# Part products of a pair interleaved with the v products of an older block

## The chip, the cores and the metric

The kernel runs on one core of a Trainium2 chip. The core has five engines, each with its own queue of instructions, which it runs in order: TensorE (PE, matrix products; PEld is its weight load), VectorE (DVE), ScalarE (ACT), GpSimd (POOL) and SyncE (SP), which issues most of the DMAs, in the order of its queue. Times are device microseconds; the metric is the median over several runs of the whole program.

## The reference

The input x has 2048 rows of 512. The result is x plus two branches on the normalized rows:

```python
xn = _layernorm(x, axis=-1)
return x + _A_ref(xn, dft matrices) + _B_ref(xn, w_q, k1, k2, u, v)
# A: y = Real(DFT_seq(DFT_hidden(xn))), by the matrices given as inputs
# B: 32 heads; each takes the best 2 of 64 x 64 = 4096 experts by product keys (k1, k2)
act = _gelu(jnp.einsum("nd,nhkd->nhk", xf, ue))      # ue = u[top_e]
out = jnp.einsum("nhk,nhk,nhkd->nd", g, act, ve)     # ve = v[top_e], g = softmax of the two scores
```

Branch B is computed densely: for every row the products with all 4096 experts, multiplied by a gate matrix that is zero except where an expert was taken.

## The kernel before, in words

The first 420 us hold branch A, the routing and the preparation of u and v (both split into two f16 parts, so that each product takes three matmuls). What the change touches begins there. It runs over 16 blocks b of 128 rows. For each block there are three kinds of work:

- **z**: the u products of the block with all 4096 experts, then gelu, into a tile of activations `act` (128 x 4096, 32 bit). Three such tiles exist, blocks take them in turn (b modulo 3).
- **G and W**: the gate. `g_prep` (lines 1283, 1288, 1291) makes one-hot factors L (1.2 us) and R (two rows of 0.4 us) on DVE for 16 of the 128 rows at a time, from a compacted table `cmp` that ACT makes from a transpose read from memory (line 948); three pairs of L and R rotate. `g_mm` (1299) multiplies them on PE, 32 matmuls for each half, two halves a G, four G a block. `w_part` (1307, 1312, 1313) multiplies activation and gate on DVE, has ACT (or, with `here=True`, DVE itself by the CAST in line 1310) round that to f16 and DVE subtract to get the second part; the result W lies in the place of the activations.
- **v**: 16 v tiles, each six matmuls of 128x512 (line 1357), all into one PSUM bank. Nine v tiles stay on the chip, seven stream through three places (`v_load`, 1333); `v_order` says in which order a block takes its 16, so that the last streamed ones serve the next block first.

Blocks 0 and 1 compute z plainly (`u_part`, 1108). From block 2 on, two blocks (a pair) share a scheme of seven products in place of eight, for each of four quads a to d of experts: 28 **slots** of 24 matmuls (1186), in the order `SEQ`. A slot "6b" is product 6 of quad b. Products 1, 6, 7 and 4 of a quad use one PSUM bank X one behind the other, 5 and 3 use Z, 2 uses Y. After each, an eviction moves or adds the bank into an activation tile: 1, 5 and 6 by ACT copies (1225, 1230, 1232), 2, 3 and 7 by DVE adds (1227, 1235, 1238), 4 by gelu on ACT (1215), with further gelus a few slots later. A slot that adds to a bank must wait for the eviction before it. Four PSUM banks are shared by all of these and by the v sums. Products 6, 3 and 7 need sums of u parts, 512 KB each, that come from memory through a **ring** of three tiles (`ring_load`, 1169). `ring_plan` decides with a model clock (1344 ns a slot) which load goes behind which slot.

The order of work is written out: `phases` is z0, z1, v0, then for each pair z(b, b+1), v(b-1), v(b), and last v15. `put(phase, place, ...)` hangs G, W, factor preparation and the rest onto places of these phases. Of the 28 slots of a pair three go into the end of v(b-2), 24 stand in a phase of their own, one goes into the start of v(b-1). Through all of this run jobs that check the input matrices: 68 **comparisons**, each two loads on SP (1395 and 1396, together 512 KB into a tile `cx`), some DVE rows from line 1411 to 1449 and sums on ACT (1382, 1385), and 35 smaller ones; they are spread over the places from place 3 (`first`) on. A scheduler then places each instruction in its engine's queue by this order and its own estimate of when inputs are there, so that an instruction of a later phase can stand ahead of one of an earlier phase. At the end of each block `finish` adds the v sum to y; `store`, `load_y` and `add_x` are its transfers. A variant called `safe` for other inputs exists and doesn't run here.

Of the kernel before, what the change touches and what calls it, by code (L numbers as in the profile page):

```python
# [18 lines left out]
P = 128  # L19
# [17 lines left out]
def tile_fnet_peer(ctx, tc, x, ca, cb, c5, wt, wf, wr, wq, kt, ut, vn, out):  # L37
# [683 lines left out]
    def part_b(safe, stS, stP, stQ, stE, xt, u_sb, cmp_p, w4):  # L721
# [471 lines left out]
        def z_pair(b, n):  # L1193
# [3 lines left out]
            total = len(SEQ) - BEFORE - BEHIND  # L1197

            def work(at):

                if at < len(SEQ):
# [3 lines left out]
                    op, qd = o[0], turn_q(o[1], n)  # L1205
# [39 lines left out]
            def middle(after):  # L1245
                cg = 0
                for k in range(total):
                    work(BEFORE + k)
                    while cg < 16 and (k + 1) * 16 >= (cg + 1) * total:
                        after(cg)  # L1250
                        cg += 1

            def behind(k):
                work(BEFORE + total + k)
                while k + 1 == BEHIND and late:
                    late.pop(0)[1]()

            return work, middle, behind
# [76 lines left out]
        def v_part(b, pv, cg):  # L1335
            w16 = parts(b)
            if b + 1 == NT and cg == 7 and not safe:
# [559 lines left out]
```

## Time and profile before

| | |
|---|---|
| median of 3 runs | 1145.69 us (1144.38 to 1147.01) |
| profiled execution | 1152.65 us, its span 1150.9 us |
| mean granted TensorE clock | 0.987 |
| z of block 0 and 1 | 418.5 to 483.5 us |
| from the first to the last v product | 483.5 to 1144.5 us |
| DMA traffic of the whole span | 220.5 MB, mean 192 GB/s |

PE is busy for 96% of the span and DVE for 83%. Busy time is a share over stages with different limits; where PE idles, the list of waits names what came last. The granted clock is 1 nearly everywhere; it is lower behind long idle times of PE. "issue" as a releaser means that the profile shows nothing that the engine waited for.

### The profile page before, as it was taken

How to read it: one execution, taken by the hardware profiler on the slowest of the kernel's cores; microseconds unless marked ns; L12 is line 12 of the kernel's file. 1: busy time of each engine (PE TensorE's matmuls, PEld its weight loads, DVE VectorE, ACT ScalarE, POOL GpSimd, SP SyncE). 2: the span in 40 equal slices, each digit the busy share in tenths (PEclk: the TensorE clock that was granted, in tenths of full speed). 3: DMA queues.
4: the chain of work that ended last, by engine and by line, in shares of the span. 5: the costliest groups of instructions: out<-in, count | busy, mean ns of one | idle time of the engine just before them, and what ended most of it. 6: DMA issues, size and time to landing. Idle time of an engine off the chain costs nothing. (4 is left out here: it accounts for less than half of the span.)

```text
span 1150.9 us, 29229 instructions
## 1 busy us (share of the span) xinstructions
PE 1109.5 (96%) x11528; PEld 724.9 (63%) x11528; DVE 959.2 (83%) x2840; ACT 682.2 (59%) x1226; POOL 333.2 (29%) x385
## 2 busy tenths in 40 slices
PE   9999999999999998599999998999998999999997
PEld 6455554544544468469569568669568659659643
DVE  7899789999989895767978877879988879879892
ACT  6558598889787582246547535546636546636530
POOL 1429999889887840000000000000000000000000
PEclk8999999999999999799999999999999999999999
DMA  9883546456344328438658656757756857747743
GB/s 299 258 222 145 191 140 218 123 196 183 112 127 129 98 82 206 122 124 285 206 187 276 198 192 232 259 176 264 230 174 231 279 177 235 256 146 235 207 129 114
DMA packets 132274, 220.52 MB, mean 192 GB/s; under 512 B 35092, under 2 KB 71067, under 8 KB 132126
## 3 DMA queue, kind: packets, MB, share of 16 engines
q1 hardware_dynamic: 129520, 214.28, 57.7%
q0 software_dynamic: 2304, 4.20, 2.3%
q8 instruction: 92, 1.51, 0.5%
q14 instruction: 56, 0.46, 0.1%
q10 hardware_dynamic: 302, 0.08, 0.0%
HBM read 183.06 MB, written 29.69 MB: 185 GB/s over the span
## 5 line engine op out<-in xcount | busy, mean ns | idle before, releaser
L252 PE MATMUL s<-m,xq 128*128 128x512 f16 x1344 | 297.4, 379 | 1.4 <-ACT ss L962 1.4
L1357 PE MATMUL v<-v,act 128*128 128x512 f16 x1044 | 233.1, 379 | 0.7 <-DVE act L1313 0.7
L252 PEld LDWEIGHTS <-xq 128*128 128x128 f16 x1344 | 129.7, 98 | 152.5 <-issue 2.7
L1370 POOL DMA_DIRECT2D y<-in_x_dram x16 | 14.4, 898 | 687.2 <-DVE L L1283 253.9
L1357 PEld LDWEIGHTS <-act 128*128 128x128 f16 x1044 | 99.3, 98 | 113.9 <-DVE act L1313 1.2
L1186 PEld LDWEIGHTS <-u 128*128 128x128 f16 x2688 | 156.5, 98 | 15.7 <-issue 9.3
L1283 DVE TENSOR_TENSOR L<-io_lam,cmp 128x2048 f16<-128x2048 f16 x128 | 154.8, 1214 | 12.1 <-PE g L1299 11.9
L966 DVE MAX8 vals<-ss 128x8 f32<-128x64 f32 x896 | 133.3, 216 | 5.5 <-ACT ss L962 5.2
L1186 PEld LDWEIGHTS <-s 128*128 128x128 f16 x1944 | 110.8, 98 | 2.2 <-DMA s<-s_d 2.1
L1357 PE MATMUL v<-v,w 128*128 128x512 f16 x480 | 107.6, 379 | 0.0
L1382 ACT ACTIVATE cx<-cx 128x896 f32<-128x896 f32 x68 | 64.3, 945 | 64.0 <-DVE cx L1430 43.9
L1312 ACT ACTIVATE act<-g 128x1024 f16<-128x1024 f32 x36 | 46.9, 1314 | 86.4 <-DVE g L1307 85.4
L970 DVE FIND_INDEX8 idx<-vals,ss 128x8 uint16<-128x256 f32 x224 | 93.8, 419 | 0.0
L962 ACT ACTIVATE ss<-s,wsc 128x512 f32<-128x512 f32 x120 | 80.2, 681 | 22.4 <-PE s L252 12.7
L1186 PE MATMUL z<-xb,u 128*128 128x128 f16 x1344 | 84.5, 219 | 5.5 <-ACT act L1215 4.5
L1186 PE MATMUL z<-x,u 128*128 128x128 f16 x1344 | 85.4, 221 | 2.2 <-DVE act L1235 1.1
L1186 PE MATMUL z<-x,s 128*128 128x128 f16 x1296 | 81.2, 219 | 1.8 <-DMA s<-s_d 1.8
L1299 PE MATMUL g<-R,L 128*128 128x32 f16 x2048 | 62.4, 176 | 20.2 <-DVE cx L1446 16.6
L1299 PEld LDWEIGHTS <-L 128*128 128x128 f16 x2048 | 60.0, 96 | 30.5 <-DVE cx L1446 16.8
L1357 PEld LDWEIGHTS <-w 128*128 128x128 f16 x480 | 45.6, 98 | 51.4
L1215 ACT ACTIVATE act<-act,scl 128x512 f32<-128x512 f32 x56 | 40.0, 719 | 54.5 <-DVE act L1235 23.6
L1307 DVE SCALAR_TENSOR_TENSOR g<-act,scl,g 128x1024 f32<-128x1024 f32 x44 | 55.8, 1281 | 11.8 <-ACT act L1215 11.8
(360 smaller groups left out, 1900.8 us busy)
## 6 DMA issues: line engine op xcount, KB each, us to landing
v<-v_d SPq DMA_DIRECT2D x67, 512.0 KB, 4.3
s<-s_d SPq DMA_DIRECT2D x63, 512.0 KB, 3.9
cx<-in_cb_dram SPq DMA_DIRECT2D x64, 448.0 KB, 6.0
w<-in_wq_dram SPq DMA_DIRECT2D x28, 512.0 KB, 5.9
fit<-in_wq_dram SPq DMA_DIRECT2D x28, 512.0 KB, 6.3
uv<-in_vn_dram SPq DMA_DIRECT2D x16, 512.0 KB
uv<-in_ut_dram SPq DMA_DIRECT2D x16, 512.0 KB, 3.6
s_d<-v SPq DMA_DIRECT2D x32, 256.0 KB, 2.5
```

Source lines behind the costliest of these rows:

```text
L252: nc.tensor.matmul(ps, xt[i][:, l, kd, :], m[:, r, kd, :], start=(n == 0), stop=(n == 3 * KD - 1))
L962: nc.scalar.activation(s, ps, AF.Copy, scale=inv)
L966: nc.vector.max(vals[:, i, w, :, h], s[:, g, :])
L970: nc.vector.max_index(idx[:, i, w].rearrange("p k h -> p (k h)"), vals[:, i, w, 0:2].rearrange("p k h -> p (k h)"), s[:, w * HC:g + 1, :]. ...
L1186: nc.tensor.matmul(bank[:, t * P:(t + 1) * P], lt, rt, start=(t == k == 0 and op in "125"), stop=(t == 3 and k == 5), skip_group_check=op ...
L1215: nc.scalar.activation(d, d if src is None else src, AF.Gelu_apprx_tanh, scale=zsc)
L1283: pin(nc.vector.tensor_tensor(L.rearrange("p t (l two) -> p t l two", two=2), io_lam.rearrange("p (l two) -> p l two", two=2).unsqueeze(1) ...
L1299: nc.tensor.matmul(p[:, hf, t * NC:(t + 1) * NC], L[:, t, :], R[:, t, :], start=True, stop=True)
L1307: nc.vector.scalar_tensor_tensor(w, act[:, :, ts], fw, w, op0=ALU.mult, op1=ALU.mult)
L1312: nc.scalar.activation(w16[..., 0], w, AF.Copy)
L1357: nc.tensor.matmul(pv, w16[:, c, :, l], v_sb[g][:, r, cc, :], start=(n + cc == 0 and k == 0), stop=(n == end and cc == 1 and k == 2))
L1382: pin(nc.scalar.activation(f, f, AF.Abs, accum_out=chk[:, n:n + 1]))
```

## The change

- `SEQ` has a new order, in which 6, 3 and 7 of a quad stand close together, and the quads are taken in one order for all pairs.
- The phases are z0, z1, then for each pair a combined phase ("a", b) with all 28 slots of the pair and, between them, the 16 v tiles of block b-2 (`TILES` says ahead of which slot each tile goes, `TILES0` for the first pair), then v(b-1); at the end v14 and v15. The first two tiles of v(b-1) go ahead of the last slot.
- The three activation tiles are allocated once. Block b+1 of a pair takes the tile of block b-2, whose v products run in the same phase; `v_order` is written so that a tile's part of `act` has been used when a slot writes there. The new order of v also changes when the streamed v tiles are loaded: v tile 9 is sixth in odd blocks.
- The model clock of the ring is 2000 ns a slot, which gives 84 loads in place of 66.
- G, W and the preparation have new places; no W uses the CAST on DVE any more. The jobs start at place 10 in place of 3, with 28 places in a combined phase and 2.2 and 2.8 us as lengths.
- `store`, `load_y`, `add_x` and the loads for the next pair (`fetch`) have new places.

The counts of PE's matmuls are the same. In the changed file most lines here are a few numbers lower (1283 is 1274, 1288 is 1279, 1291 is 1282, 1299 is 1290, 1307 is 1298, 1357 is 1352, 1333 is 1324, 1413 is 1407); 1169 is 1170.

```diff
+        AT = [a.tile([P, NC, P], F32, tag="act", name=f"act{n}") for n, a in enumerate(ap)]
+        AT.append(w4.rearrange("p (c n) -> p c n", n=P))
+
         def act_tile(b):
-            if b % 3 == 2:
-                return w4.rearrange("p (c n) -> p c n", n=P)
-            return ap[b % 3].tile([P, NC, P], F32, tag="act", name=f"act{b}")
-
-        BT = [act_tile(b) for b in range(2)]
+            return AT[b % 3]
+
...
-            SEQ = ("1a 5a 2a 6a 1b 3a 2b 7a 5b 6b 1c 4a 3b 7b 2c 5c 6c 1d 4b 3c 7c 5d 2d 6d 4c 3d 7d 4d").split()
-            BEFORE, BEHIND = 3, 1
-
-            def turn_q(k, n):
-                return ((0, 3, 2, 1), (1, 3, 2, 0))[n % 2]["abcd".index(k)]
+            SEQ = ("1a 5a 2a 6a 3a 7a 1b 4a 5b 2b 6b 3b 7b 1c 4b 5c 2c 6c 3c 7c 1d 4c 5d 2d 6d 3d 7d 4d").split()
+            TILES = [1, 2, 3, 3, 4, 6, 8, 10, 11, 13, 15, 17, 18, 20, 22, 24]
+            TILES0 = [0, 0, 0, 0, 0, 0, 0, 1, 3, 5, 8, 11, 14, 17, 20, 23]
+
+            def turn_q(k):
+                return (0, 3, 2, 1)["abcd".index(k)]
...
-                    ns = 1344
+                    ns = 2000
                     if OPS[o[0]][1] is not None:
-                        USES.append((clock, clock + ns, turn_q(o[1], n), OPS[o[0]][1]))
+                        USES.append((clock, clock + ns, turn_q(o[1]), OPS[o[0]][1]))
                     clock += ns
-                clock += 50000
+                clock += 22000
...
+                    if at + 1 == len(SEQ):
+                        while late:
+                            late.pop(0)[1]()
+
+            return work
...
-        VO = [None if n in (1, 3, 5, 7, 9, 12, 14) else 0 for n in range(16)]
-        res, ext = iter(range(V2)), iter(range(V2, 16))
-        VO = [next(ext if v is None else res) for v in VO]
-
         def v_order(b):
-            return VO if b % 2 else VO[::-1]
+            if b % 2:
+                return [15, 13, 11, 7, 6, 9, 5, 4, 3, 2, 1, 0, 8, 14, 12, 10]
+            if b < 14:
+                return [10, 12, 14, 8, 0, 1, 2, 3, 4, 5, 6, 7, 9, 11, 13, 15]
+            return [10, 12, 14, 8, 0, 1, 2, 9, 3, 4, 5, 6, 7, 11, 13, 15]
...
+            for n in (2 * cg, 2 * cg + 1):
+                v_tile(b, pv, n)
+
+        def v_tile(b, pv, n):
+            w16 = parts(b)
             end = 13 if b + 1 == NT and not safe else 15
-            for n in (2 * cg, 2 * cg + 1):
-                g = v_order(b)[n]
-                for cc in range(2):
-                    c = 2 * g + cc
-                    for k, (l, r) in enumerate(((0, 0), (0, 1), (1, 0))):
-                        nc.tensor.matmul(pv, w16[:, c, :, l], v_sb[g][:, r, cc, :], start=(n + cc == 0 and k == 0),
-                                         stop=(n == end and cc == 1 and k == 2))
-
-                if g >= V2 and g not in [v for v in v_order(b) if v >= V2][-3:]:
-                    v_load(PL[g])
+            g = v_order(b)[n]
+            for cc in range(2):
+                c = 2 * g + cc
+                for k, (l, r) in enumerate(((0, 0), (0, 1), (1, 0))):
+                    nc.tensor.matmul(pv, w16[:, c, :, l], v_sb[g][:, r, cc, :], start=(n + cc == 0 and k == 0),
+                                     stop=(n == end and cc == 1 and k == 2))
+            if g >= V2 and g not in [v for v in v_order(b) if v >= V2][-3:]:
+                v_load(PL[g])
-        phases = [("z", 0), ("z", 1), ("v", 0)]
-        for b in range(2, NT, 2):
-            phases += [("z", b, b + 1), ("v", b - 1), ("v", b)]
-        phases += [("v", 15)]
+        phases = [("z", 0), ("z", 1)]
+        for b in PAIRS:
+            phases += [("a", b), ("v", b - 1)]
+        phases += [("v", 14), ("v", 15)]
...
-        for b in range(NT):
-            ph = ("v", b)
-            if b % 2 == 0 and 0 < b < 13:
-                nx = phases[phases.index(ph) + 1]
-                st = 1 if len(nx) == 2 else 2
-                put(("v", b - 1), 7, LRP(b + 1, 0))
-                put(ph, 1, G(b + 1, 0), LRP(b + 1, 1, 0))
-                put(ph, 2, LRP(b + 1, 1, 1))
...
-                put(nx, st, W(b + 1, 2, True), G(b + 1, 3))
-                put(nx, 3 * st, W(b + 1, 3, True))
...
+        for b in PAIRS:
+            o, ph, nx = b - 1, ("a", b), ("v", b - 1)
+            put(("v", o - 2) if o > 1 else ("z", 1), 7, LRP(o, 0))
+            put(ph, 1, G(o, 0), LRP(o, 1, 0))
+            put(ph, 2, LRP(o, 1, 1))
+            put(ph, 4, G(o, 1), LRP(o, 2, 0))
+            put(ph, 5, LRP(o, 2, 1))
+            put(ph, 6, W(o, 0))
+            put(ph, 9, G(o, 2), LRP(o, 3, 0), W(o, 1))
+            put(ph, 10, LRP(o, 3, 1))
+            put(ph, 13, G(o, 3), W(o, 2))
+            put(ph, 17, W(o, 3))
+            put(ph, 3, lambda b=b: compact_d(b))
+            put(ph, 20, LRP(b, 0))
+            put(ph, 24, G(b, 0), LRP(b, 1, 0))
+            put(ph, 25, LRP(b, 1, 1), G(b, 1))
+            put(ph, 26, LRP(b, 2, 0))
+            put(nx, 1, LRP(b, 2, 1), W(b, 0))
+            put(nx, 2, W(b, 1))
+            put(nx, 3, G(b, 2), LRP(b, 3))
+            put(nx, 4, W(b, 2), G(b, 3))
+            put(nx, 6, W(b, 3))
+            if b < 14:
+                put(nx, 3, lambda o=o: compact_d(o + 2))
...
         if not safe:
-            slots = [(ph, cg) for ph in phases[2:] for cg in range(16 if len(ph) == 3 else 8)][:-5]
+            slots = [(ph, cg) for ph in phases[2:] for cg in range(28 if ph[0] == "a" else 8)][:-5]
             at = [0.0]
             for ph, cg in slots:
-                at.append(at[-1] + (2.1 if ph[0] == "z" else 3.0))
+                at.append(at[-1] + (2.2 if ph[0] == "a" else 2.8))
...
-            first = 3
+            first = 10
...
+            for b in PAIRS:
+                put(("a", b), 27, timed(store, b - 2))
+                put(("v", b - 1), 1, timed(load_y, b - 1))
+                put(("v", b - 1), 4, timed(add_x, b - 1))
+                nx = ("a", b + 2) if b < 14 else ("v", 14)
+                put(nx, 1, timed(store, b - 1))
+                put(nx, 3, timed(load_y, b))
+                put(nx, 6 if b < 14 else 5, timed(add_x, b))
+            put(("v", 15), 1, timed(store, 14))
...
+        def fetch(b):
+            for c in (b, b + 1):
+                prep(c)
+            if not safe:
+                nc.sync.dma_start(x4.rearrange("p l o k n -> p (l o k n)"), t_d[b // 2])
+
+        def end_v(b, pv, pvt):
+            if safe:
+                load_y(b)
+                add_x(b)
+            finish(b, pv)
+            if safe:
+                store(b)
+            banks.append(pvt)
+
+        def both(b):
+
+            if b == 2:
+                ring_load(-1)
+                fetch(b)
+                if not safe:
+                    for k in "abcd":
+                        first_sum(turn_q(k))
+            for c in (b, b + 1):
+                ACT[c] = act_tile(c)
+            pv, pvt = take(f"v{b - 2}")
...
+            work = z_pair((b, b + 1), b // 2 - 1)
+            n = 0
+            for k in range(len(SEQ)):
+                while n < 16 and (TILES if b > 2 else TILES0)[n] <= k:
+                    v_tile(b - 2, pv, n)
+                    n += 1
+                    if n == 16:
+                        end_v(b - 2, pv, pvt)
+                if k + 1 == len(SEQ):
+                    nx = take(f"v{b - 1}")
+                    for m in range(2):
+                        v_tile(b - 1, nx[0], m)
+                work(k)
+                hooks(("a", b), k)
+            return nx
+
...
+            if ph[0] == "a":
+                begun = both(b)
+                continue
+            pv, pvt = begun or take(f"v{b}")
             for cg in range(8):
...
+                if cg == 1 and b % 2 and b < 13:
+                    fetch(b + 3)
```

How the change moves rows, at three places. First DVE's queue at the end of z1, where the last G of block 0 gets its factors (L_5774 and the R tiles; `cx_6989` is the tile of the first comparison). Before:

```order
L1288 TENSOR_TENSOR R_5773<-io_c,cmp_5716 128x512
L1413 SCALAR_TENSOR_TENSOR cx_6989<-cx_6989,not_79 128x256
L1291 TENSOR_TENSOR R_5773<-R_5773,cmp_5716 128x512
L1413 SCALAR_TENSOR_TENSOR cx_6989<-cx_6989,not_79 128x256
L1415 TENSOR_TENSOR cx_6989<-cx_6989 1x256
L1430 TENSOR_TENSOR cx_6989<-cx_6989 1x2x63
L1432 TENSOR_TENSOR cx_6989<-cx_6989 1x1
L1444 TENSOR_TENSOR cx_6989<-cx_6989,c_239 1x128
L1283 TENSOR_TENSOR L_5774<-io_lam,cmp_5716 128x2048
L1307 SCALAR_TENSOR_TENSOR g_2_6448<-act_5781,scl,g_2_6448 128x32x32
```

and now:

```order
L1279 TENSOR_TENSOR R_5773<-io_c,cmp_5716 128x512
L1282 TENSOR_TENSOR R_5773<-R_5773,cmp_5716 128x512
L1274 TENSOR_TENSOR L_5774<-io_lam,cmp_5716 128x2048
L1298 SCALAR_TENSOR_TENSOR g_2_6448<-act_5781,scl,g_2_6448 128x32x32
L1279 TENSOR_TENSOR R_5775<-io_c,cmp_5716 128x512
L1279 TENSOR_TENSOR R_5777<-io_c,cmp_5720 128x512
```

The comparison's rows between R and L are gone from here; its first rows now stand in the first combined phase.

Second, DVE's queue in the second pair from the add of product 3 of the first quad to the add of product 7 of the same quad. Before:

```order
L1235 TENSOR_TENSOR w_126<-z_4_1_8463,w_126 128x4x128
L1227 TENSOR_TENSOR act_8415<-z_4_3_8663,act_8415 128x4x128
L1424 TENSOR_TENSOR cx_8630<-cx_8630 128x768
L1291 TENSOR_TENSOR R_5777<-R_5777,cmp_8377 128x512
L1238 TENSOR_TENSOR w_126<-z_4_1_8416,act_8415 128x4x128
```

and now:

```order
L1235 TENSOR_TENSOR w_126<-z_4_0_8258,w_126 128x4x128
L1274 TENSOR_TENSOR L_5774<-io_lam,cmp_8102 128x2048
L1279 TENSOR_TENSOR R_5777<-io_c,cmp_8102 128x512
L1279 TENSOR_TENSOR R_5773<-io_c,cmp_8102 128x512
L1238 TENSOR_TENSOR w_126<-z_4_0_8224,act_5782 128x4x128
```

An add of the next quad and a row of a comparison between the two adds give way to an L and two R rows.

Third, SP's queue at the border of the first combined phase and v1, as it is now (`s` is the ring, `v` a streamed v tile):

```order
L1170 DMA s_2_9_7803<-s_d 128x2048
L1170 DMA s_3_10_7868<-s_d 128x2048
L1389 DMA cx_7914<-in_ca_dram 128x128
L1390 DMA cx_7914<-in_cb_dram 128x896
L1170 DMA s_1_11_7941<-s_d 128x2048
L1324 DMA v_1_7956<-v_d 128x2048
L1324 DMA v_1_7964<-v_d 128x2048
```

Three ring loads and a comparison's loads stand ahead of the two loads of v tiles; in the old order the rows at this border are loads of comparisons, of x and of v tiles, and none of the ring.

More of the change, by code (lines that the diff above doesn't have):

```diff
@@ L1243, in work @@
                         banks.append(Xt)
[L1245 to L1258, printed above, removed]
+                    if at + 1 == len(SEQ):
+                        while late:
+                            late.pop(0)[1]()
+            return work
         GP = {}
@@ L1599, in W @@
             return lambda: w_part(b, k, here)
-        if not safe:
-            for n in range(len(QUADS)):
-                put(("v", 0), n, lambda qd=turn_q("abcd"[n], 0): first_sum(qd))
         put(("z", 0), 5, G(0, 0))
@@ L1646, in part_b @@
[L1646 to L1648 removed]
+        put(("v", 14), 1, LRP(15, 2), W(15, 0))
+        put(("v", 14), 2, W(15, 1))
+        put(("v", 14), 3, G(15, 2), LRP(15, 3, 0))
+        put(("v", 14), 4, LRP(15, 3, 1), W(15, 2), G(15, 3))
+        put(("v", 14), 6, W(15, 3))
         if not safe:
[L1650 removed]
+            slots = [(ph, cg) for ph in phases[2:] for cg in range(28 if ph[0] == "a" else 8)][:-5]
@@ L1702, in part_b, with hooks @@
[L1702 to L1731 removed]
+        def hooks(ph, cg):
+            for f in plan.get((ph, cg), ()):
+                f()
```

106 lines of the change are left out of this document (25 added, 81 removed).

## The prediction

> **What bounds the kernel now.** I read the busy shares first, then the list of waits, then the timeline around the longest wait of PE, then the windows by stage.
>
> ```profile
> PE 1109.5 (96%) x11528; PEld 724.9 (63%) x11528; DVE 959.2 (83%) x2840; ACT 682.2 (59%) x1226; POOL 333.2 (29%) x385
> ```
>
> PE is busy for 1109.5 of 1150.9 us, and the change leaves its matmuls as they are. So the change can gain only where PE stands idle or runs slowly, and it can lose wherever DVE, at 83%, comes late. The list of waits has one item on PE that is far longer than all others:
>
> ```profile
> PE g L1299 <- DVE cx L1446: 16.6, 1, 16.6
> DVE cx L1413 <- issue: 14.1, 1, 14.1
> ```
>
> It is one G (the gate product) that waited 16.6 us, once, and DVE itself had stood still for 14.1 us of that in a line of the matrix comparison. The timeline shows the place, the end of the stage that computes z of block 1:
>
> ```profile
> 441.55 8.20 PE L1108 MATMUL z<-xb,u 128*128 128x128 f16 x144
> ...
> 450.39 5.52 PE L1108 MATMUL z<-xb,u 128*128 128x128 f16 x96
> 452.73 0.33 SPq L1396 DMA_DIRECT2D cx<-in_cb_dram  x1
> ...
> 464.06 0.48 DVE L1413 SCALAR_TENSOR_TENSOR cx<-cx,not 128x256 f32<-128x256 f32 x1 [14.10 <-issue]
> 464.46 0.42 DVE L1291 TENSOR_TENSOR R<-R,cmp 128x512 f16<-128x512 f16 x1
> ...
> 466.28 1.21 DVE L1283 TENSOR_TENSOR L<-io_lam,cmp 128x2048 f16<-128x2048 f16 x1
> ...
> 471.23 1.21 DVE L1283 TENSOR_TENSOR L<-io_lam,cmp 128x2048 f16<-128x2048 f16 x1
> 472.49 1.03 PE L1299 MATMUL g<-R,L 128*128 128x32 f16 x32 [16.59 <-DVE cx L1446]
> 473.37 9.54 PE L1108 MATMUL z<-xb,u 128*128 128x128 f16 x144
> ```
>
> PE ends its z product at 455.91 and gets the next G only at 472.49. The comparison's second load (448 KB) was issued at 452.73; the first read of the tile runs at 464.06, and everything behind it in DVE's queue, the one-hot factors L and R of this G among them, stands until then. After the wait the same 144 matmuls take 9.54 us, before it 8.20.
>
> The rest of the program is in the windows (columns: us; busy time and instructions of PE, PEld, DVE, ACT, POOL; granted clock; DMA share; GB/s):
>
> ```profile
> 455.90:472.50 16.60, 0.01 (x2) 0.01 (x1) 8.28 (x16) 1.86 (x3) 0.00 (x0) 0.60 0.72 126
> 472.50:483.50 11.00, 11.00 (x207) 11.00 (x208) 7.38 (x10) 4.64 (x6) 0.00 (x0) 0.83 0.26 70
> 483.50:1144.50 661.00, 647.18 (x8148) 463.25 (x8144) 540.16 (x900) 342.44 (x648) 14.41 (x17) 1.00 0.65 210
> ```
>
> From 483.5 (the first v product) to 1144.5 (the last) PE is idle for 661.00 − 647.18 = 13.8 us at full clock. So there are two amounts to win: 16.6 + 1.3 us in one place, and at most about 14 spread over fourteen blocks. Who ended the second:
>
> ```profile
> PE z L1186 <- ACT act L1215: 4.5, 2, 2.5
> PE g L1299 <- DVE R L1291: 3.0, 5, 1.3
> PE z L1186 <- DVE act L1235: 1.9, 5, 0.6
> PE z L1186 <- DMA s<-s_d: 1.8, 2, 1.1
> PE z L1186 <- DVE w L1235: 0.9, 1, 0.9
> PE v L1357 <- DVE act L1313: 0.7, 1, 0.7
> PE g L1299 <- DVE L L1283: 0.4, 1, 0.4
> PE z L1186 <- DVE w L1227: 0.2, 1, 0.2
> ```
>
> **Part 1, the first comparison leaves the z stage.** With the first job at place 10 in place of 3 of the slot list, and the order of DVE shown above, L1413's rows are gone from between the two halves of R of this G; they come in the first combined stage. What then sets the G: its R and L rows, which in the old order stood behind the comparison. DVE was free from 464.06 − 14.10 = 449.96. After the wait it needed from 464.46 to the end of the last L, 471.23 + 1.21 = 472.44, so 7.98 us, of which the comparison's own rows took the 1.4 between the R row's end (464.88) and the first L (466.28). Without them 6.6 us from 449.96 on give 456.5, 0.6 us after PE's 455.91. ACT's copy of the compacted tile may come later, as it waits for a transpose from memory: bounds 0 and 2 us. I leave 1.0 us of stall in all. Without the long stand the restart costs nothing: −(9.54 − 8.20) = −1.3. Part 1: −16.6 − 1.3 + 1.0 = **−16.9 us**. If only the wait went and the slow restart stayed, it would be −15.6.
>
> The Trainium skill ("TensorE: Matmul & The Clock Gate", section "What's actually happening") says that an idle window of about 3.4 us halves the clock and that a window of work restores it; half of 3.4 us is an estimate of 1.7 us for the restart where the row shows 1.3. By it the sum would be 0.4 us lower; the row is used. The granted clock of 0.60 and 0.83 in the two windows agrees with the rule.
>
> **Part 2, the ring of sums.** The three ring tiles are reloaded 84 times in place of 66: 18 more loads of 512 KB, each by an SP issue. They lie beside PE's work while the transfers keep up:
>
> ```profile
> v<-v_d SPq DMA_DIRECT2D x67, 512.0 KB, 4.3
> s<-s_d SPq DMA_DIRECT2D x63, 512.0 KB, 3.9
> ...
> DMA to landing us min/median/max: 3.4/3.9/6.4
> ```
>
> (The last row is that of the ring's load line.) 18 × 0.5 MB more than the 210 GB/s × 661 us = 139 MB of this stretch makes 148 MB, in about 650 us 228 GB/s; the busiest stretch now, the middle of a pair, ran at 257:
>
> ```profile
> 597.70:633.30 35.60, 34.66 (x678) 34.55 (x675) 31.13 (x51) 25.16 (x51) 0.00 (x0) 1.00 0.79 257
> ```
>
> What matters more is the lead. A ring load goes out behind the slot that used the tile last. Counting the slots between that and the next use in the two written orders: now 28 loads have five slots between and 35 have six. A slot issues in 1.33 us (597.70 to 599.03 in the rows below), so that is 6.7 and 8.0 us, against landings of up to 6.4 plus their queue. In the new order one load has 6.7, and all others 8.0 to 17 us (18 of them reach over a stage border), since v tiles of 1.29 us (six of them, 36 matmuls, from 486.94 to 494.70) lie between. The last two rows are what late ring loads cost today:
>
> ```profile
> 486.94 7.93 PE L1357 MATMUL v<-v,act 128*128 128x512 f16 x36
> 494.70 0.95 PE L1299 MATMUL g<-R,L 128*128 128x32 f16 x32
> ...
> 597.70 1.50 PE L1186 MATMUL z<-x,s 128*128 128x128 f16 x24
> ...
> 599.03 1.50 PE L1186 MATMUL z<-xb,u 128*128 128x128 f16 x24
> ...
> 699.94 1.51 PE L1186 MATMUL z<-x,s 128*128 128x128 f16 x24 [0.69 <-DMA s<-s_d]
> ...
> 703.93 1.87 PE L1186 MATMUL z<-xb,u 128*128 128x128 f16 x24 [2.48 <-ACT act L1215]
> ```
>
> The 2.48 follows the 0.69 by one ACT queue that had stood; so I count the 4.5 us of L1215 with the 1.8 of the ring: 6.3 us. Bounds after: 0 and 6.3. I take 1.5.
>
> **Part 3, slots closer together.** In one quad the slots 1, 6, 7, 4 use one PSUM bank (X), and each must wait for the eviction of the one before. Until now three slots lay between 6 and 7 and between 7 and 4 (4.0 us); in the new order there is one slot and one v tile or G, 1.33 + 1.29 = 2.62 less the 0.17 by which a slot's 1.50 outlasts its issue: about 2.45 us. How late evictions are, in two quads (the first slot is the 597.70 above; the rows of each quad stand in order of time):
>
> ```profile
> 599.23 0.60 ACT L1232 ACTIVATE w<-z 128x512 f32<-128x512 f32 x1 [0.62 <-PE z L1186]
> 603.05 1.50 PE L1186 MATMUL z<-x,s 128*128 128x128 f16 x24
> 606.83 0.69 DVE L1238 TENSOR_TENSOR w<-z,act 128x512 f32<-128x512 f32 x1
> ...
> 535.48 1.50 PE L1186 MATMUL z<-x,s 128*128 128x128 f16 x24
> ...
> 539.87 0.69 DVE L1238 TENSOR_TENSOR act<-z,w 128x512 f32<-128x512 f32 x1
> ```
>
> Slot 6 ends at 599.20 and its copy at 599.83: 0.6 us, no wait. Slot 7 ends at 604.55 and its add at 607.52: 3.0 us; and at 536.98 and 540.56: 3.6. With 2.45 us of cover these two would stall PE by 0.5 and 1.1. Over 28 quads that is 0 to 31 us; today's waits for these adds (L1235, L1227) are 1.9 + 0.9 + 0.2 = 3.0. DVE also loses work: no W takes the CAST any more,
>
> ```profile
> L1310 DVE CAST act<-g 128x1024 f16<-128x1024 f32 x8 | 10.4, 1296 | 0.0
> ```
>
> (and four more on the other tile), 12 × 1.3 = 15.6 us that go to ACT, busy for 342 of 661 us. The late adds stood behind a comparison's row on DVE. I take 0.5 us in every third quad, 5 us, so +2.0 against today.
>
> **Part 4, G and W.** Waits for R, L and the subtraction were 3.0 + 0.4 + 0.7, with 0.4 unnamed: 4.5. G now lies farther from its factors in a longer stage, but W in the odd block must end before v tiles; I take 3.5.
>
> **Part 5, the new v order.** In odd blocks v tile 9 is loaded behind the block's first tile and used as its sixth: one slot and four v tiles, 1.33 + 4 × 1.29 = 6.5 us, against 4.3 median with ring and comparison loads ahead of it in SP's queue (order of SP above). Bounds 0 and 7 × 2 us; I take 1.
>
> Idle of parts 2 to 5: 1.5 + 5 + 3.5 + 1 = 11.0 against 13.8: **−2.8 us**.
>
> **The sum.** −16.9 − 2.8 = −19.7. The profiled execution took 1152.65 us, so 1133 for it; the median of the three unprofiled runs is 1145.69, 6.96 less, and the same difference gives **1126 us**. Should those 6.96 us sit in the very stall, 7 of the 16.9 are not there to win, and it is 1133.
>
> **Rivals.**
> *All stalls vanish.* If the tiles between slots cover every eviction, the 13.8 us go whole: 1145.69 − 16.9 − 1.0 − 13.8 = 1114. For it: leads of 8 us and more. Against: adds that are 3 us late.
>
> *Transfers are late.* Seven odd blocks wait for v tile 9 or a ring load by about 1 to 2 us: 7 to 14 us over the forecast, 1133 to 1140. For it: the comparison's second load took this long where DMA was crowded,
>
> ```profile
> DMA to landing us min/median/max: 3.2/5.6/10.4
> ```
>
> (the row of line L1395). Against: in the middle of a pair DMA was busy to 0.79 only. The Trainium skill ("DMA: Bandwidth & Descriptors", section "Queues, rings and completion order") says that descriptors of one ring are consumed in order, so that tile 9's load would stand behind the ring and comparison loads issued before it; no row here separates that from a busy memory.
>
> *The stall only moves.* The change then doesn't do what its first part says. The first comparison now stands in the first combined stage, again ahead of one-hot rows on DVE. If its loads land as late as the 10.4 us above, DVE stands some 5 to 12 us and PE with it: 1131 to 1138. Against it: by then the transfers have fallen to 70 GB/s (the second window above), and the comparison's rows stand 8 us and more behind its loads in the plan.
>
> *The slots are too close, the slower side.* Its place is the bank X of each quad, its price 0.5 to 1.1 us for each late add. Forecast and before lie 20 us apart, so from 20/28 = 0.7 us more in every quad it is no gain. At 1.1 for one need in each quad: 28 × 1.1 = 31 in place of my 5, 1152. Against it: only in quads with a comparison ahead on DVE were the adds that late.
>
> **How the numbers follow.** Forecast 0.56; all stalls vanish 0.13; late transfers 0.12; the stall moves 0.10; slots too close 0.09. The likeliest gives 1126, its own range 1119 to 1133. The range reaches from 1114, where all is won, to 1140, where two of the middle cases lie; left out are most of the last case and the ends of the others. About 0.2% (2.3 us) is what a measurement of this kernel can tell from no change. Faster: 0.55 + 0.13 + 0.11 + 0.08 = 0.87; the same takes 0.05 of the tails, slower 0.08, nearly all of it from the slots.
>
> **What would show it.** Right: no wait of PE over 3 us before the first v product; z's 144 matmuls at 8.2 us throughout; no line of PE waiting for DMA s over 2 us in sum; PE's waits for L1238's and L1235's successors at about 5 us; idle of PE from the first to the last v product near 11. Part 1 is wrong if the wait before v of block 0 stays above 5 us or turns up in the first combined stage; part 2 if s, part 5 if v tiles are what PE waits for; part 3 if the adds of slot 7 end most waits and their sum is over 10 us. The whole is wrong if PE's busy time itself grows, as by a lower granted clock.

## The result and the profile after

The changed kernel took 1139.29 us (median of 5 runs, 1138.36 to 1140.89), the kernel before beside it 1145.28 (5 runs, 1144.12 to 1147.01). The ratio is 0.995 with a 95% interval of 0.9936 to 0.9965. So it is faster by 6 us, where 20 were forecast. Two later series, on two chips, gave 0.990 (0.9880 to 0.9924) and 0.994 (0.9914 to 0.9965).

The profiled execution of the changed kernel took 1138.36 us. Its busy shares, from the page:

```profile
PE 1107.2 (97%) x11528; PEld 722.0 (64%) x11528; DVE 943.8 (83%) x2828; ACT 695.9 (61%) x1238; POOL 332.6 (29%) x385
```

DVE has lost 15.4 us of work and ACT has gained 13.7, which fits the twelve CASTs that went from DVE to ACT. The waits of PE from the first v product to the last:

```profile
PE g L1290 <- DVE L L1274: 4.6, 8, 1.3
PE g L1290 <- DVE R L1282: 3.2, 4, 1.0
PE z L1187 <- DVE w L1238: 2.9, 3, 1.8
PE z L1187 <- ACT w L1215: 1.8, 2, 1.3
PE v L1352 <- DVE w L1304: 0.9, 1, 0.9
PE v L1352 <- DVE act L1304: 0.7, 1, 0.7
PE v L1352 <- DMA v<-v_d: 0.5, 1, 0.5
PE z L1187 <- DVE act L1238: 0.3, 1, 0.3
PE v L1352 <- ACT act L1303: 0.2, 1, 0.2
```

The waits for the ring have gone, those for L and R have grown. The timeline of the same place in z of block 1 that held the long wait:

```profile
450.53 0.43 DVE L1282 TENSOR_TENSOR R<-R,cmp 128x512 f16<-128x512 f16 x1
...
450.93 5.52 PE L1108 MATMUL z<-xb,u 128*128 128x128 f16 x96
...
455.88 1.21 DVE L1274 TENSOR_TENSOR L<-io_lam,cmp 128x2048 f16<-128x2048 f16 x1
457.14 0.96 PE L1290 MATMUL g<-R,L 128*128 128x32 f16 x32 [0.69 <-DVE L L1274]
...
463.06 4.58 PE L1108 MATMUL z<-xb,u 128*128 128x128 f16 x79 [1.32 <-issue]
...
467.49 2.75 PE L1352 MATMUL v<-v,act 128*128 128x512 f16 x12
```

The second R row follows at once where a comparison's row had stood for 14 us, and the G waits 0.69 us in place of 16.59. Behind it PE stops once for 1.32. The program in two windows, from the start of z to the first v product and from there to the last; the kernel before first, the changed kernel below:

```profile
418.50:483.50 65.00, 48.41 (x928) 48.24 (x927) 43.14 (x121) 26.58 (x34) 5.45 (x3) 0.87 0.54 134
```

```profile
419.00:467.50 48.50, 46.49 (x898) 46.10 (x897) 41.35 (x113) 25.81 (x33) 5.45 (x3) 1.00 0.67 159
467.50:1130.00 662.50, 646.95 (x8175) 461.89 (x8172) 527.01 (x895) 356.79 (x660) 14.41 (x17) 1.00 0.69 226
```

The z stages take 16.5 us less. A part of this is no gain: the first G of block 1, 32 matmuls in 0.95 us, stood in the first window and stands in the second now (x928 and x898 matmuls of PE). The v stages take 662.5 us where they took 661.0, with 662.5 − 646.95 = 15.6 us of idle PE where there were 13.8.

That makes 14.3 us between the two profiled executions (1152.65 and 1138.36), but 6.0 between the medians. The difference lies mostly in the kernel before: its profiled execution was 7.4 us above its median, the changed kernel's 0.9 below its own. So there are two questions: what is a usual execution of the kernel before, and why have the v stages not become shorter.

### The profile page after: what moved, and what is told of

The parts are those of the page before. It is cut to its first block, busy times and chain, and to the rows that moved or that the text cites. A ratio compares the mean times of both kernels' runs of the same rounds, so it can differ in the third digit from the quotient of the medians.

```text
span 1136.3 us, 29241 instructions
## 1 busy us (share of the span) xinstructions
PE 1107.2 (97%) x11528; PEld 722.0 (64%) x11528; DVE 943.8 (83%) x2828; ACT 695.9 (61%) x1238; POOL 332.6 (29%) x385
## 5 line engine op out<-in xcount | busy, mean ns | idle before, releaser
L1352 PE MATMUL v<-v,act 128*128 128x512 f16 x1044 | 241.4, 379 | 1.1 <-DVE act L1304 0.7
L1352 PE MATMUL v<-v,w 128*128 128x512 f16 x480 | 111.1, 379 | 1.4 <-DVE w L1304 0.9
L1303 ACT ACTIVATE act<-g 128x1024 f16<-128x1024 f32 x44 | 57.7, 1311 | 61.8 <-DVE g L1298 61.8
L1215 ACT ACTIVATE act<-act,scl 128x512 f32<-128x512 f32 x56 | 40.2, 720 | 53.0 <-DVE act L1235 27.9
L1304 DVE TENSOR_TENSOR act<-g,act 128x1024 f16<-128x1024 f32 x44 | 57.3, 1301 | 13.9 <-ACT act L1303 13.5
```

Of the source, the lines that this page charges most:

```text
L1215: nc.scalar.activation(d, d if src is None else src, AF.Gelu_apprx_tanh, scale=zsc)
L1303: nc.scalar.activation(w16[..., 0], w, AF.Copy)
L1304: nc.vector.tensor_tensor(w16[..., 1], w, w16[..., 0], op=ALU.subtract)
L1352: nc.tensor.matmul(pv, w16[:, c, :, l], v_sb[g][:, r, cc, :], start=(n + cc == 0 and k == 0), stop=(n == end and cc == 1 and k == 2))
```

## The experiments

Runs e1 to e4 and e9 to e12 were taken on one chip, where the kernel before took 1146.63 us both times; e5 to e8 on another (1147.34). "z" below is the time from the start of z to the first v product, "v" from there to the last, both from the one profiled execution of each run.

| run | median us (runs) | ratio to before, 95% | z | v |
|---|---|---|---|---|
| kernel before, first profile | 1145.28 (5) | | 65.0 | 661.0 |
| e1 kernel before again | 1146.87 (10) | 1.0009 (0.9993 to 1.0025) | 64.0 | 656.6 |
| changed kernel, first | 1139.29 (5) | 0.995 (0.9936 to 0.9965) | 48.5 | 662.5 |
| e6 changed kernel again | 1137.46 (6) | 0.9902 (0.9880 to 0.9924) | 47.0 | 663.4 |
| e10 changed kernel again | 1140.91 (7) | 0.994 (0.9914 to 0.9965) | 48.9 | 664.9 |
| e3 changed, first job 3 | 1155.36 (5) | 1.0079 (1.0061 to 1.0096) | 63.0 | 666.1 |
| e2 before, first job 10 | 1136.52 (5) | 0.9901 (0.9883 to 0.9918) | 49.2 | 660.2 |
| e12 the same again | 1134.84 (5) | 0.9902 (0.9881 to 0.9923) | 48.8 | 662.3 |
| e8 before, first job 5 | 1135.94 (6) | 0.9892 (0.9869 to 0.9915) | 49.0 | 663.7 |
| e9 before, early jobs alone moved | 1132.48 (5) | 0.9888 (0.9867 to 0.9909) | 48.0 | 658.2 |
| e4 changed, one G later | 1133.10 (6) | 0.9894 (0.9871 to 0.9917) | 48.3 | 657.5 |
| e11 the same again | 1131.60 (6) | 0.9889 (0.9866 to 0.9912) | 46.9 | 659.2 |
| e5 changed, two G later | 1134.99 (6) | 0.9878 (0.9849 to 0.9908) | 48.7 | 659.8 |
| e7 changed, 12 CASTs back | 1137.01 (6) | 0.9905 (0.9886 to 0.9924) | 48.1 | 665.4 |

### e1: the kernel before, profiled once more

No edit.

> The kernel before, unchanged, for a second profiled execution. Theory A (the long wait in the z stage of block 1 is about 8 us shorter in executions without the profiler than the 16.6 us that the profile shows, and that is why 1152.65 us profiled stands against 1145.3): profiled again at about 1152 with a wait of 15 to 17 us, unprofiled 1145. Theory A2 (the length of that wait differs from execution to execution): profiled anywhere between 1140 and 1153, its wait between 5 and 17 us and the difference of the totals that of the waits. Theory B (the wait is 16.6 us in every execution, and the 7 us lie elsewhere): the wait 16.6 us, whatever the total.

Ten executions took 1143.96 to 1153.57 us; the profiled one was among the fast ones, 1145.56. Its windows:

```profile
416.90:480.90 64.00, 49.02 (x930) 48.83 (x929) 43.25 (x121) 26.68 (x34) 5.46 (x3) 0.87 0.53 136
480.90:1137.50 656.60, 645.34 (x8146) 461.55 (x8141) 540.26 (x900) 342.22 (x648) 14.39 (x17) 1.00 0.66 212
```

and its longest waits of PE, of the whole span and of the v stages:

```profile
PE g L1299 <- DVE cx L1446: 15.0, 1, 15.0
```

```profile
PE z L1186 <- ACT act L1215: 3.7, 2, 2.4
PE g L1299 <- DVE R L1291: 3.0, 5, 1.3
PE z L1186 <- DVE w L1235: 1.3, 1, 1.3
PE z L1186 <- DVE act L1235: 1.3, 4, 0.5
```

The long wait is 15.0 us, nearly the whole of the 16.6. So theory A (the wait is 8 us shorter in a usual execution) falls, and so does A2 (the wait makes the difference of the totals): the z stages make only 1.0 us of the 7.1 between the two. Theory B is the nearest: the wait is nearly the same, and the rest lies elsewhere. 4.4 us lie in the v stages (661.0 and 656.6; idle 13.8 and 11.3), 1.6 in the part ahead of z (which starts at 418.5 and 416.9). 1152.65 was an execution near the upper end of what this kernel does.

Against this second execution the changed kernel's first profile (1138.36) is 7.2 us shorter: 15.5 less in z, but 5.9 more in v (0.95 of it the G that moved) and 2.1 more ahead of z. So beside a usual execution the v stages have become longer, with 15.6 us of idle PE in place of 11.3.

### e3: the wait brought back into the changed kernel

```diff
-            first = 10
+            first = 3
```

> The changed kernel with the first job at place 3 again; the first comparison's rows then stand in DVE's queue of the z stage of block 1, between the rows of the same R. Theory A: the wait is back, profiled 1138.4 + 16 = about 1154, unprofiled 1139.3 + 8 = about 1147, so slower than the kernel before. Theory B: unprofiled 1155. If the comparison isn't the cause: 1139.

1155.36 us, 16.1 above the changed kernel's first median and 14.5 above that of e10 on the same chip. The wait is back:

```profile
PE g L1290 <- DVE cx L1440: 14.7, 1, 14.7
```

So it is the comparison's rows on DVE that hold this G, and the whole wait counts, in the medians too: theory B's number (1155), not A's (1147). z is 63.0 us, 14 to 16 more than in the three profiles of the changed kernel; the v stages, 666.1, are longer too, as the line moves nearly all jobs and not only the first. The changed kernel with this wait is 9 us slower than the kernel before with it.

### e2, e8, e12: the first job later in the kernel before

```diff
-            first = 3
+            first = 10
```

(5 in e8.)

> The kernel before with the first job at place 10 in place of 3, so that the first comparison's rows are no longer in DVE's queue of the z stage; nothing else. Theory A: profiled 1152.65 - 17 = about 1136, unprofiled 1145.3 - 17 + 8 = about 1136 to 1137, so this one line gives more than the whole change (1139.3). Theory B: unprofiled 1128 to 1129. If the comparison isn't what holds DVE there: 1145.

> The kernel before with the first job at place 5 (3 before, 10 in the run that gave 1136.5). The comparison's rows are out of the z stage here too, but all comparisons stand elsewhere among the G of the later stages. Theory P (the wait in z is the whole gain, 15 to 16 us, and the run with 10 gave back about 4 to 6 us because its comparison rows came between the rows of R: 6.9 us of waits for R against 3.0): between 1130 and 1137, the difference to 1136.5 being that of the waits for R and L. Rival (the line is worth 10 us wherever the jobs start): 1136 to 1137 with waits for R near 3.

> The kernel before with the first job at place 10, again, beside the changed kernel on one chip: whether the rest of the change (other than that line) gains, loses or does nothing. By the traces so far (v stages 660.2 here, 662.6 and 663.4 in the changed kernel) it loses 0 to 3 us: the median 0 to 3 us below the changed kernel's.

This one line gave 1136.52 and 1134.84 us (10) and 1135.94 (5): as much as the whole change or more. On the chip where both ran, the changed kernel (e10, 1140.91) is 6.1 us above e12 in the medians, more than expected; the intervals of their ratios, 0.9914 to 0.9965 and 0.9881 to 0.9923, just overlap, and the two profiled executions are 3.0 apart (1140.91 and 1137.91). The 1136.5 is theory A's number, but not for its reason; theory B's 1128 to 1129 was not reached, because the v stages grew. z is 15 us shorter, but the v stages, 656.6 and 661.0 before, are 660.2 to 663.7. In e12 PE waits there for

```profile
PE g L1299 <- DVE R L1291: 6.8, 7, 1.9
PE z L1186 <- DVE act L1235: 2.6, 3, 1.3
```

where before it was 3.0 for R; in e8 it is 6.1, so e8's rival, with waits for R near 3, falls. The line moves nearly all jobs against the G, not only the first: by the program text by seven places at the start of the list (10 in place of 3) and fewer and fewer towards its end. What stands between the two rows of an R is not a comparison's row, as e8's text has it. In all the waits for R of e12, e8 and e9 it is the first row of a W (1307, 1.28 us); here is one of e12:

```profile
983.69 1.28 DVE L1307 SCALAR_TENSOR_TENSOR g<-act,scl,g 128x1024 f32<-128x1024 f32 x1
984.88 0.41 DVE L1291 TENSOR_TENSOR R<-R,cmp 128x512 f16<-128x512 f16 x1
985.35 0.55 PE L1299 MATMUL g<-R,L 128*128 128x32 f16 x16 [1.49 <-DVE R L1291]
```

The comparisons come in further ahead. Four places make the difference between e12 and e9 (the next run, which leaves most comparisons where they were): PE waits there 1.30, 0.41, 1.49 and 1.86 us in e12 and 0, 0, 0.51 and 1.13 in e9. At the first, second and fourth, rows of a comparison stand between the two L of this G in e12 and not in e9; at the third, the one shown, a comparison's row ahead of both L had stood 0.74 us for its load.

### e9: only the early jobs later

```diff
-                s0 = max(when(free[m % CB]), first + m * (len(slots) - first - 6) // len(jobs))
+                s0 = max(when(free[m % CB]), first + m * (len(slots) - first - 6) // len(jobs), 10)
```

> The kernel before in which only the jobs that would start ahead of place 10 are put back to it; all later ones keep their places, so DVE's rows behind the first pair stand as in the kernel before. Theory P (the wait in z is worth 15 to 16 us; the runs with first 10 and 5 gave back 4 to 6 of it because all comparisons moved against the G): from the start of z to the first v product 48 to 49 us (63 to 65 before), the v stages 656 to 658 us with waits for R near 3, the median 15 us below before's, ratio 0.987. Rival (without the wait something else in the v stages becomes late, wherever the comparisons are): v stages 660 to 664, ratio 0.990 as with first 10.

1132.48 us, 14.2 below the kernel before; z 48.0, v stages 658.2, and the longest waits are near those of the kernel before:

```profile
PE z L1186 <- ACT act L1215: 4.2, 2, 2.5
PE g L1299 <- DVE R L1291: 3.5, 6, 1.1
```

By the program text the first jobs move, by up to seven places, with some of those that wait for the same `cx` tiles, and all later ones stay. Theory P holds in the trace: z is 16 to 17 us shorter, the v stages are within 2 to 3 us of the two profiles of the kernel before and 0.2 over what P said, and the waits for R are half of what they are when nearly all comparisons move. The medians don't settle the size: the interval of e9's ratio holds P's 0.987 and the rival's 0.990, and e9 is 2.4 us below e12 with overlapping intervals, where z also starts 2.0 us earlier in e9's profile (416.9 and 418.9), ahead of everything that was edited.

### e4, e11: one G later in the changed kernel

```diff
-            put(ph, 25, LRP(b, 1, 1), G(b, 1))
-            put(ph, 26, LRP(b, 2, 0))
+            put(ph, 25, LRP(b, 1, 1))
+            put(ph, 27, G(b, 1), LRP(b, 2, 0))
```

> The changed kernel with the second G of each even block behind the pair's last slot in place of two slots ahead of it, so some 4 us later; L and R are prepared where they were. Theory G (in the changed kernel this G stands one slot behind the G before it, and its second L can be written only when that one has been read): the 4.6 us of PE's waits for L, at one place in each pair, go under 1 us, unprofiled about 1135.5. Rival (DVE is simply late there, and the next G or the add of slot 7 waits in its place): 1138 to 1140 with the same sum of waits in other rows.

> The changed kernel with the second G of each even block behind the last slot, again, beside the unchanged one. Theory G: no waits for L over 1 us in sum, v stages 657 to 659, the median 4 to 5 us below the changed kernel's. If the medians agree within 1.5 us, the waits for L were replaced by others.

1133.10 and 1131.60 us. On one chip and in one series the median of e11 is 9.3 us below that of the unchanged e10; by the ratios to the kernel before (0.994 and 0.9889) it is about 6. The waits of PE in the v stages, first of e10, then of e11:

```profile
PE g L1290 <- DVE R L1282: 4.4, 4, 1.4
PE g L1290 <- DVE L L1274: 4.2, 6, 1.2
PE z L1187 <- DVE w L1238: 2.3, 2, 2.0
```

```profile
PE g L1290 <- DVE R L1282: 3.1, 5, 0.9
PE z L1187 <- DVE w L1238: 2.0, 1, 2.0
```

The waits for L are gone and the v stages are 5.7 us shorter (664.9 to 659.2); PE's idle time in them goes from 16.3 to 11.2. Why the waits were there is seen in the timeline of the changed kernel at one such place (a G is 32 matmuls, 16 for each half; the 32 for each half that the words on the kernel before name are those of a whole G):

```profile
786.59 0.88 DVE L1407 SCALAR_TENSOR_TENSOR cx<-cx,not 128x256 f32<-128x256 f32 x2 [4.37 <-issue]
...
789.52 0.95 PE L1290 MATMUL g<-R,L 128*128 128x32 f16 x32
...
790.89 1.21 DVE L1274 TENSOR_TENSOR L<-io_lam,cmp 128x2048 f16<-128x2048 f16 x1
...
792.16 0.56 PE L1290 MATMUL g<-R,L 128*128 128x32 f16 x16 [0.33 <-DVE L L1274]
...
793.04 0.41 DVE L1405 TENSOR_TENSOR cx<-cx 128x256 f32<-128x256 f32 x1
...
793.57 0.67 DVE L1235 TENSOR_TENSOR act<-z,act 128x512 f32<-128x512 f32 x1
...
794.17 1.20 DVE L1274 TENSOR_TENSOR L<-io_lam,cmp 128x2048 f16<-128x2048 f16 x1
...
795.43 0.57 PE L1290 MATMUL g<-R,L 128*128 128x32 f16 x16 [1.15 <-DVE L L1274]
```

and of e4, at the same place, where everything comes 3.2 us earlier (its first row is the L that stands at 794.17 above):

```profile
790.94 1.20 DVE L1274 TENSOR_TENSOR L<-io_lam,cmp 128x2048 f16<-128x2048 f16 x1
...
794.34 0.95 PE L1290 MATMUL g<-R,L 128*128 128x32 f16 x32
```

In the changed kernel the two halves of this G come 2.6 and 5.9 us behind the G ahead of it. From 790.89 on DVE has, without a pause, an L, two R rows, a comparison's rows, the add of slot 3 and the second L to do; that L ends when PE has waited 1.15. In e4 the G comes 2.2 us after the end of the same L. One half of my reason falls: the L row has no idle time ahead of it, so here it was not held by its buffer but stood behind other rows. A comparison has its part in this place, the worst of the seven: its row at 786.59 ends 4.37 us in which DVE stood still. In e4 DVE stands still at the same row, for 4.21 us, and PE doesn't wait, as its G comes later.

The medians move by 6 and 9 us where the waits for L are 4 to 5. The profiled executions show where the rest lies. From the changed kernel's first profile to e4 it is 6.1 us: 5.0 in v, 0.2 in z and 0.8 ahead of z. From e10 to e11 it is 9.9: 5.7 in v, 2.0 in z and 2.3 ahead of z, where nothing was edited. So by these profiles the moved G is worth 5 to 6 us; the 9 is in part luck.

### e5: a second G later

As e4, and

```diff
-            put(nx, 4, W(b, 2), G(b, 3))
+            put(nx, 4, W(b, 2))
+            put(nx, 5, G(b, 3))
```

> As the kernel with the second G of each even block behind the last slot, and the fourth G of that block one place (two v tiles) later, so that the second R of its factors, which stood behind a comparison's rows on DVE, is ready. Theory G (PE's waits for L and R are all a matter of how far a G stands behind the one before it): the 3.3 us of waits for R go under 1 us, 2 to 3 us less than 1133.1, so about 1130.5. Rival (comparison rows make DVE late wherever a G stands): no less than 1132.

1134.99 us, not 1130.5; v stages 659.8. It ran on another chip than e4, and the interval of its ratio (0.9849 to 0.9908) doesn't tell it from e4's, so the trace decides: PE is idle for 13.8 us of the v stages, in e4 for 11.4. The waits for R are 2.2 us in place of 3.3, but others take their place:

```profile
PE g L1290 <- DVE R L1282: 2.2, 2, 1.6
PE v L1352 <- DMA v<-v_d: 2.2, 3, 1.3
PE z L1187 <- ACT w L1215: 1.8, 2, 1.1
PE g L1290 <- DVE L L1274: 1.6, 1, 1.6
```

Here the rival is right: not every wait for L or R goes by moving the G.

### e6, e10: the changed kernel again

> The changed kernel again, unchanged, beside the others on one chip. Expected 1138 to 1141, its v stages (first to last v product) 662 to 664 us, where a second execution of the kernel before had 656.7 and the first 660.9. If it falls under 1136, single executions and not the change explain a part of the difference between it and the others.

> The changed kernel a third time, on the same chip as the three others. The ratio to before was 0.995 and 0.990 on two chips; expected 0.990 to 0.995, v stages 662 to 664 us.

1137.46 and 1140.91 us, v stages 663.4 and 664.9: e6's time is half a microsecond under what was expected, e10's v stages are one above. The v stages of the changed kernel are 662.5 to 664.9 in three executions, against 656.6 and 661.0 in two of the kernel before; 0.95 us of the difference is the G that moved.

### e7: the CAST on DVE again

```diff
-            put(ph, 13, G(o, 3), W(o, 2))
-            put(ph, 17, W(o, 3))
+            put(ph, 13, G(o, 3), W(o, 2, o > 2))
+            put(ph, 17, W(o, 3, o > 2))
```

> The changed kernel with the CAST on DVE again for the last two W of six odd blocks, 12 in all, as the kernel before had it. In the changed kernel DVE stands 18 us in all waiting for ACT's copy of W (7 us before). Theory: these waits are not on the path; 12 x 1.3 us more on DVE and 12 waits of some 0.6 us less change nothing or cost up to 2 us: 1139 to 1141. Rival (they are what makes L and R late for PE): 3 us and more less, under 1136.5.

1137.01 us beside 1137.46 (e6, on the same chip): no difference that these runs could show. In the changed kernel DVE had waited for ACT's copy (first lines), and with the CASTs back PE still waits for L (second):

```profile
DVE act L1304 <- ACT act L1303: 12.0, 23, 2.9
...
DVE w L1304 <- ACT w L1303: 6.1, 8, 1.4
```

```profile
PE g L1290 <- DVE L L1274: 4.0, 6, 1.3
```

DVE's own waits for ACT's copy, 12.0 + 6.1 = 18 us, are 9.6 + 3.1 = 12.7 in e7, and PE's idle time in the v stages is 16.5 us in e6 and in e7. So these waits are not what makes L late, and the move of the CASTs to ACT is worth too little to be seen.

## Why the prediction was right or wrong

**The direction was right, the size was wrong by a factor of three**, and the time lies at the upper edge of the range, which was set there by rivals (late transfers, a stall that moves) that did not come as described: that it lies inside is luck. Two steps failed, by about 8 and about 6 us; smaller errors of other terms offset a part.

*The step from the profiled execution to the median failed.* The sum, −19.7, was made against 1152.65 us and then carried to the median with "the same difference". Against the changed kernel's profiled execution the sum was off by 5.4 (forecast 1133, measured 1138.36); the other 8.3 us come from this step. A profiled execution is one of a set that spreads from 1144 to 1153.6 (e1), and 1152.65 lay at its end. Of its surplus of 7.1 us over the second execution 4.4 lay in the v stages, 1.8 of it longer busy time of PE and 2.5 idle time (13.8 and 11.3 us). This idle time I counted as something that the change could remove, and then took the surplus off once more; the same holds for the 1.6 us by which the wait was longer. I did name the case that the surplus sits in the wait, and gave 1133 for it; e1 shows only those 1.6 us there. The changed kernel's profile lay 0.9 us under its median, the other way, and that is chance.

*Part 1 was right in its mechanism and nearly in its size.* Forecast −16.9; z became 16.5 us shorter in the two profiles, 0.95 of it the G that moved, and 14 to 18 in any pair of kernels with and without the wait (63.0 to 65.0 against 46.9 to 49.2). The stall left over was 0.69 + 1.32 = 2.0 us where I left 1.0. Behind the wait the 65 and 79 matmuls of z took 3.79 and 4.58 us, 8.4 in all, where 144 had taken 9.54, and the granted clock of this window is 1.00 in place of 0.87. By the Trainium skill ("TensorE: Matmul & The Clock Gate", section "What's actually happening") an idle window of about 3.4 us throttles the clock; the two waits that are left are shorter, and the trace agrees.

*Part 2, the ring:* forecast 6.3 to 1.5 us. The waits for the ring are 0, those for L1215, which the prediction counted here, 1.8. That the new order did it is not shown: in e12, with the old order, the two are 0.8 and 1.2 us, in e9 0.5 and 4.2. The loads themselves take longer now (the page's rows of after: `s` 4.9 us in place of 3.9, `v` 5.5 in place of 4.3):

```profile
s<-s_d SPq DMA_DIRECT2D x81, 512.0 KB, 4.9
v<-v_d SPq DMA_DIRECT2D x67, 512.0 KB, 5.5
```

at 226 GB/s where 228 was the estimate, and no slot waited for them.

*Part 3, slots closer together:* forecast 3.0 to 5 us, measured 2.9 + 0.3 = 3.2 in the waits for L1238, the add of slot 7, and none for L1235 and L1227. So bank X now makes slots wait for the add that the prediction named, at four places and not in every third quad, and in sum it is no more than the adds cost before. The rival of slots too close (1152 and more) did not come.

*Part 4, G and W, is the term that was mis-sized:* forecast 4.5 to 3.5, measured 4.6 + 3.2 + 0.9 + 0.7 + 0.2 = 9.6 us, 6.1 too little. The step was the sentence that G "now lies farther from its factors in a longer stage". It was said for all G and worked out for none. The second G of each even block stands nearer: one slot behind the first, with adds and comparison rows between its factors on DVE. In the third pair it starts 2.1 us behind the first G (702.35 and 704.49), where in the kernel before five slots and 7.5 us lay between (710.92 and 718.42). e4 and e11 show it by moving this one G by two slots and two v tiles: the waits for L, 4.6 of the 9.6 us, vanish, and the v stages lose 5.0 and 5.7 us. The waits for R, 3.2, stay near 3 in both, and e5 didn't remove them as a whole. At all four places the first row of a W (1298, 1.28 us) stands between the two rows of the R; what it would give to put it behind them was not tried.

*Part 5, v tile 9:* forecast 1 us; PE waited once for a v tile, 0.5 us. The rival of late transfers did not decide; 2.2 us were the most, in e5.

*The rival "the stall only moves"* is refuted for z. Something near it is true in a way I had not thought of: the line that takes the first comparison out of z moves nearly all of them, and at four places their rows then make DVE late with an R (6.8 us of waits for R in e12, 3.5 in e9).

What the change is made of, then: its gain is the one line on the first job. That line alone gives 10 to 12 us in the kernel before, and 14 in the median if only the early jobs move (e9). With the rest of the change, the common stage of part products and v products, the waits for the ring are gone and those for L and R take as much or more; with the one G moved it comes to 1131.6 to 1133.1, level with e9's 1132.5.

## What to carry to other kernels

Make the sum against more than one execution: here the profiled one, 7 us above the median, had 2.5 us more idle time in the v stages than the next, and what one execution has too much is not to be won twice. When a constant shifts one job out of a bad place, look at what it does to all the others in the same queue; move the one alone first. When work is interleaved, check for each product how long its factors have since the product before it, on the engine that makes them, and not for the stage as a whole.

## What was not expected

Executions of one and the same program on one chip differ by up to 0.8%: 1143.96 to 1153.57 us in ten of the kernel before, 1135.38 to 1142.61 in seven of the changed kernel. The prediction held 2.3 us for enough to tell two kernels apart; the medians of the changed kernel in three series lie 3.4 us apart (1137.46 to 1140.91). Differences of 2 to 3 us between medians of five could not be told apart here; the time of the stages and the sums of waits in the traces could.

One part of the spread can be placed. z starts at 416.4 to 420.5 us in the fourteen profiles, and the two of the kernel before, one program, are 1.6 us apart there. In the four in which it starts before 417 (e1, e7, e9, e11) the granted clock in the first 20 us of the program is 1.00, in the ten others, with z at 418.2 and later, 0.76 to 0.83. These are the first 20 us of e10, then of e11, in the columns of the windows above:

```profile
0.00:20.00 20.00, 18.14 (x92) 13.23 (x93) 13.11 (x43) 11.99 (x26) 2.44 (x20) 0.83 0.89 304
```

```profile
0.00:20.00 20.00, 17.99 (x113) 13.74 (x113) 13.45 (x45) 12.37 (x28) 2.44 (x20) 1.00 0.86 307
```

With 113 matmuls done in place of 92, e11 is ahead of e10 long before the first line that was edited. A comparison of totals takes this in; one from the start of z on doesn't.

And the ratio of the same two programs was 0.995, 0.990 and 0.994 in three series, of which the last two ran on different chips; the intervals of the first two (0.9936 to 0.9965, 0.9880 to 0.9924) do not meet. What differs between the series no run shows.
